# Retention and two feed-forwards on one core: attention of the later blocks split into early and late queries

## The chip, the cores and the metric

The kernel runs on one core of one Trainium2 chip. The metric is the time of one execution on the device in microseconds; a smaller number is better. TensorE multiplies matrices into PSUM, VectorE (DVE) and ScalarE (ACT) work element by element, GpSimd (POOL) does so too but has no access to PSUM, and SyncE (SP) issues the transfers between HBM and SBUF.

## The reference

Four sequences of 576 positions, 8 heads of 64 columns. First comes retention: scores of each query with each earlier key, weighted by a power of a head's gamma that falls with the distance, with no softmax. Its result goes through two feed-forwards over all 2304 positions.

```
scores = q @ k.T / sqrt(64)
Dmat   = where(i >= j, gamma[h] ** (i - j), 0)      # i query, j key
x      = (scores * Dmat) @ v                        # heads side by side: 2304 x 512
h      = x @ w_in;  x = (max(h, 0) + alpha * min(h, 0)) @ w_out          # 512 -> 2048 -> 512
y      = (sigmoid(x @ w_gate) * (x @ w_val)) @ w_out2                    # 512 -> 1536 -> 512
```

Everything is float32 to the reader. The change touches the retention alone.

## The kernel before, in words

**Blocks and chunks.** The 2304 positions are cut into five blocks (`BLOCKS`, L28: 256 positions and four times 512). A sequence is cut at multiples of 128 positions and at the borders of blocks; the pieces are the chunks (`CHUNKS`, L74 to L89), of 128 positions or, at a few borders, 64. Retention is done chunk by chunk. Within a chunk the queries meet the chunk's own keys (the scores); all earlier chunks of the sequence are held in a state of 64 x 64 for each head (`m_sb`), which every chunk reads and then updates.

**A chunk.** Head `2 * pr + e` has its 64 query and key columns in the upper or lower half of the partitions, by `e`; there are four pairs `pr`. GpSimd first scales the queries by powers of gamma (`att_q`, L527) and the values by inverse powers (`att_v`, L535), so that the decay needs no further work. Then TensorE does, as 8 products each:

- the scores (`att_scores`, L571): 128 keys against 128 queries over 64 partitions, so that two heads share the array by rows; VectorE multiplies the two PSUM tiles by the causal mask, once for each `e` (L574);
- the state update `m` (L597): keys times values, into a PSUM tile of its own; VectorE adds it to `m_sb` and scales (L608, L609); left out in the last chunk of a sequence;
- the queries times the old state (L600), into two PSUM tiles `o`; left out in the first chunk of a sequence;
- the masked scores times the values (L611), added into the same `o` tiles.

ScalarE and VectorE then copy `o` to the input `x_t` of the feed-forward. In the trace each of these products is two instructions, so 8 products are 16. Chunks of 64 positions keep two heads in each tile and take a path of their own (L555 for the scores).

**Tiles in PSUM.** From the third block on the two score tiles and the two `o` tiles of a chunk have the same two tags, `a` and `b`, of a pool with one buffer each (`ps_a`): `o` may be written once VectorE has masked the scores. The state update uses the pool `ps_h`, which it shares with the feed-forward.

**Where the chunks stand.** The first two blocks are done in one run at the start (`att_run`), with another pool and one VectorE multiplication for both halves (L564). The chunks of the third to fifth block are put between the steps of the first feed-forward: the main loop takes one stage of `att_stages` at a time, scores and then the rest, with 12 or more matmuls of the feed-forward in between (`for j in range(1, PLAIN)`, L1268). The 13 chunks of these blocks are done from 141 to 264 us; 11 of them have 128 positions. Beside that, VectorE and ScalarE prepare weights for the second feed-forward.

**The order of the work.** TensorE executes in the order in which the program issues (`manual_schedule`, L1493). For the other engines and SyncE's transfers a planner sets the order from its own estimates (`schedule_with_timeline_sim`, L1492); each engine then works strictly in that order. So GpSimd's scaling for a chunk often runs one or two chunks ahead of TensorE, as its load lands.

**Constants.** One array `cst` holds the scaling of the queries, the 128 x 128 mask, the inverse powers, and a 64-wide mask for short chunks, each at a column offset `O_...` (L93 to L98); it is the first load of the program (L502).

Of the kernel before, what the change touches and what calls it, by code (L numbers as in the profile page):

```python
# [10 lines left out]
F32 = mybir.dt.float32  # L11
# [4 lines left out]
ALU = mybir.AluOpType  # L16
# [3 lines left out]
P = 128  # L20
B, H, S, D = 4, 8, 576, 64
NPAIR = H // 2
NT = B * S
DM = 512
# [73 lines left out]
N_CST = O_GK2 + NPAIR  # L98


def constants():
    gamma = (1.0 - 2.0 ** (-5.0 - np.arange(H, dtype=np.float32))).astype(np.float64)
    i = np.arange(P)
    head = 2 * np.arange(NPAIR)[None, :] + (i // D)[:, None]
    out = np.zeros((P, N_CST), np.float32)
    out[:, :O_M] = (gamma[head][:, :, None] ** i / np.sqrt(D)).reshape(P, -1)
    out[:, O_M:O_GK] = i[None, :] >= i[:, None]
    out[:, O_GK:O_GP] = gamma ** -i[:, None].astype(np.float64)
    out[:, O_GP:O_M2] = (gamma[head][:, None, :] ** np.array(LENGTHS)[None, :, None]).reshape(P, -1)

    out[:, O_M2:O_GK2] = i[None, :D] >= i[:, None] % D
    out[:, O_GK2:] = gamma[head] ** -(i[:, None] % D).astype(np.float64)
    return out

# [2 lines left out]
def retention_two_ffn(ctx: ExitStack, tc: tile.TileContext, att, cst, alpha, w1, w2, out0, out1):  # L117
    nc = tc.nc

    const = ctx.enter_context(tc.tile_pool(name="const", bufs=1))  # L120

    big = ctx.enter_context(tc.tile_pool(name="big", bufs=1))
    small = ctx.enter_context(tc.tile_pool(name="small", bufs=2))
# [15 lines left out]
    m_sb = ap.tile([P, NPAIR, D], F32, tag="m", name="m_sb")  # L139
    c_sb = ap.tile([P, N_CST], F32, tag="c", name="c_sb")  # L140
# [21 lines left out]
    mask = c_sb[:, O_M:O_GK]  # L162
    decay = c_sb[:, :O_M].rearrange("p (a i) -> p a i", a=NPAIR)


# [221 lines left out]
    second = []  # L387
# [94 lines left out]
    o = 0  # L482
    for n, (_, _, _, c, _) in enumerate(CHUNKS):
        offset[n] = o
        o += 4 * c * H * D

    def load_chunk(n):
        if n >= len(CHUNKS) or n in raw_a:
            return
        load_qk(n)  # L490
        load_kv(n)

    def load_qk(n):
        if n >= len(CHUNKS):
            return
        c = CHUNKS[n][3]
        half = 2 * c * H * D
# [11 lines left out]
    def load_kv(n):  # L509
        if n >= len(CHUNKS):  # L510
            return
# [17 lines left out]
    def att_v(n):  # L529

        v = raw_a[n][1][:, 1]
        heads = v.shape[1]
        gk = O_GK if heads == H else O_GK2
# [10 lines left out]
    def att_scores(n, pool, tags):  # L544

        c = CHUNKS[n][3]
        qk = raw_a[n][0]
        if c < P:
            if len(tags) == 1:
                ps = pool.tile([P, 2, DM], F32, tag=tags, name=f"s{n}")[:, 0, :NPAIR * c]  # L550
                ps = ps.rearrange("p (a i) -> p a i", a=NPAIR)
            else:
                ps = pool.tile([P, NPAIR, c], F32, tag=tags[0], name=f"s{n}")
            for pr, e in HEADS:
                nc.tensor.matmul(ps[part(e), pr, :], qk[part(e), 1, pr, :], qk[part(e), 0, pr, :], start=True, stop=True)  # L555
            by = c_sb[:, O_M2:O_GK2].unsqueeze(1).to_broadcast([P, NPAIR, c])
            nc.vector.tensor_tensor(out=qk[:, 1], in0=ps, in1=by, op=ALU.mult)
            return qk[part(0), 1], qk[part(1), 1]
        if len(tags) == 1:
            ps = pool.tile([P, 2, DM], F32, tag=tags, name=f"s{n}")  # L560
            for pr, e in HEADS:
                nc.tensor.matmul(ps[:, e, pr * P:(pr + 1) * P], qk[part(e), 1, pr, :], qk[part(e), 0, pr, :], start=True, stop=True)
            s_sb = both_scores[n] = slot([P, 2, NPAIR, P], F32, f"sc{n}")
            nc.vector.tensor_tensor(  # L564
                out=s_sb.rearrange("p e a i -> p (e a) i"), in0=ps.rearrange("p e (a i) -> p (e a) i", a=NPAIR),
                in1=mask.unsqueeze(1).to_broadcast([P, H, c]), op=ALU.mult,
            )
            return s_sb[:, 0], s_sb[:, 1]
        ps = [pool.tile([P, NPAIR, P], F32, tag=tags[e], name=f"s{n}_{e}") for e in range(2)]
        for pr, e in HEADS:  # L570
            nc.tensor.matmul(ps[e][:, pr, :], qk[part(e), 1, pr, :], qk[part(e), 0, pr, :], start=True, stop=True)  # L571
        s_sb = qk[:, 1], small.tile([P, NPAIR, P], F32, tag="s", bufs=3, name=f"sc{n}")
        for e in (1, 0):
            nc.vector.tensor_tensor(  # L574
                out=s_sb[e], in0=ps[e], in1=mask.unsqueeze(1).to_broadcast([P, NPAIR, c]), op=ALU.mult,
            )
        return s_sb

    def att_values(n, s_sb, pool, tags):
# [13 lines left out]
        rows = lambda t, pr, e: kv[part(e), t, pr] if c < P else kv[:, t, 2 * pr + e]  # L593
        if not last:
            m_ps = ps_h.tile([P, NPAIR, D], F32, tag="h", name=f"m{n}")
            for pr, e in HEADS:
                nc.tensor.matmul(m_ps[part(e), pr, :], rows(0, pr, e), rows(1, pr, e), start=True, stop=True)  # L597
        if pos:
            for pr, e in HEADS:
                nc.tensor.matmul(  # L600
                    out(pr, e), m_sb[part(e), pr, :], qk[part(e), 0, pr, :], start=pr < 2, stop=False,
                )
# [7 lines left out]
        for pr, e in HEADS:  # L610
            nc.tensor.matmul(  # L611
                out(pr, e), rows(1, pr, e), s_sb[e][:, pr, :], start=pos == 0 and pr < 2, stop=pr >= 2,
            )
# [606 lines left out]
    late = []  # L1220
# [38 lines left out]
    n = runs_of(2)[0]  # L1259
# [8 lines left out]
    for j in range(1, PLAIN):  # L1268
# [5 lines left out]
        for f in range(first, NF1):  # L1274
# [4 lines left out]
            if j == PLAIN - 1 and staged == total:  # L1279
                if not under_left:  # L1280
# [38 lines left out]
    pool = ctx.enter_context(tc.tile_pool(name="wide", bufs=1, side="right", reuse_waits="tile"))  # L1319
# [110 lines left out]
    ps = [ps_y.tile([P, DM], F32, tag="y", name=f"o0_{e}") for e in range(BLOCKS[0] // P)]  # L1430
    last = None
    for f in range(NF2):
# [4 lines left out]
        g = plain_z(f, ws.pop(f))  # L1437
# [59 lines left out]
```

## Time and profile before

| | us |
|---|---|
| median of 3 runs | 863.33 (863.12 to 864.38) |
| profiled execution | 862.71 |
| its span, first to last instruction | 860.9 |
| TensorE busy in the span | 844.4 |
| VectorE busy | 547.9 |
| ScalarE busy | 419.7 |
| GpSimd busy | 97.3 |

The span is that of the profiled execution; what lies around it is start and end of the program. Busy time is the union of an engine's instructions. Matmuls overlap, so the wall time from the first instruction of a group to the first of the next is what counts in a dense stretch.

### The profile page before, as it was taken

The page shows a single profiled execution, that of the slowest core. Times are in us where ns is not written, and L with a number is a line of the kernel's source. Part 1 is how long each engine was busy: PE and PEld are TensorE (multiplying, and loading weights), DVE is VectorE, ACT ScalarE, POOL GpSimd, SP SyncE. Part 2 cuts the span into 40 slices and gives each one's busy share as a digit, 9 for nine tenths or more (in the row PEclk, how much of TensorE's full clock was granted, in tenths as well). Part 3 has the DMA queues.
Part 4 walks back from the last instruction along what each step waited for, and adds up shares of the span by engine and source line. Part 5 has one row for each costly group of instructions (what it writes and reads, how often), then busy time and mean ns, then how long its engine had stood idle before and what let it go on. Part 6 is the DMA issues. An engine that isn't in the chain of part 4 may idle for free.

```text
span 860.9 us, 13167 instructions
## 1 busy us (share of the span) xinstructions
PE 844.4 (98%) x4898; PEld 704.9 (82%) x4898; DVE 547.9 (64%) x840; ACT 419.7 (49%) x724; POOL 97.3 (11%) x72
## 2 busy tenths in 40 slices
PE   6899999999999999999999999999999999999998
PEld 5798888777778887888888888888888888888897
DVE  4899863785786969997647675469813332695111
ACT  1777754453564769986336653345412222352111
POOL 5357623223100000000000000000000000000000
PEclk9999999999999999999999999999999999999999
DMA  9658999699977125899967999255896561569970
GB/s 341 228 186 274 348 402 365 221 358 407 417 263 280 49 91 194 294 364 346 409 222 274 411 417 407 103 196 192 294 394 228 187 199 69 172 223 371 366 285 26
DMA packets 81728, 234.04 MB, mean 272 GB/s; under 512 B 8576, under 2 KB 9600, under 8 KB 81664
## 3 DMA queue, kind: packets, MB, share of 16 engines
q1 hardware_dynamic: 81664, 233.20, 73.9%
q8 instruction: 39, 0.64, 0.3%
q14 instruction: 25, 0.20, 0.1%
HBM read 169.72 MB, written 63.44 MB: 271 GB/s over the span
## 4 chain that ended last, share of the span: by engine, by line
PE 78%; DVE 1%; DMA 1%; ACT 1%; issue 0%; SPq 0%; DVEq 0%; ACTq 0%
PE a L700 15%; PE yy L700 10%; PE oa L700 8%; PE y L700 6%; PE h L700 5%; PE a_h L700 5%; PE z L700 4%; PE c L700 4%; PE b L700 4%; PE e L700 4%; PE o L700 2%; PE oc L700 2%; PE ob L700 2%; PE oe L700 2%; PE b_h L700 1%; PE c_h L700 1%
## 5 line engine op out<-in xcount | busy, mean ns | idle before, releaser
L700 PE MATMUL h<-x,w 128*128 128x512 f32 (+1 forms) x432 | 84.1, 346 | 2.1 <-DVE t L720 1.3
L700 PEld LDWEIGHTS h<-x,w 128*128 128x128 f32 x432 | 67.5, 190 | 12.6 <-DVE t L720 1.9
L700 PE MATMUL y<-g,w 128*128 128x512 f32 x240 | 58.9, 394 | 0.0
L336 ACT ACTIVATE q<-r 128x512 fp32r<-128x512 f32 x72 | 45.2, 664 | 24.3 <-PE yy L700 9.1
L231 POOL TENSOR_SCALAR r<-r 128x512 int32<-128x512 uint32 x26 | 51.9, 1996 | 42.2 <-DMA r<-w 30.1
L337 DVE TENSOR_TENSOR q<-r,q 128x512 fp32r<-128x512 f32 x72 | 49.3, 709 | 9.7 <-ACT q L336 9.7
L716 ACT ACTIVATE t<-h 128x512 f32<-128x512 f32 (+1 forms) x48 | 25.0, 521 | 57.8 <-PE h L700 57.8
L700 PEld LDWEIGHTS y<-g,w 128*128 128x128 f32 x240 | 44.4, 188 | 10.2 <-issue 1.0
L1029 DVE TENSOR_TENSOR c<-a,es 128x512 f32<-128x512 f32 x24 | 16.7, 699 | 55.3 <-PE a L700 55.3
L229 ACT ACTIVATE r<-r 128x512 f32<-128x512 f32 x68 | 45.0, 669 | 8.2 <-DMA r<-w 6.3
L238 DVE CUSTOM_DVE_ANT_0 r<-r,top 128x1024 uint16<-128x1024 uint16 x52 | 35.6, 696 | 2.3 <-POOL r L231 0.5
L700 PEld LDWEIGHTS z<-x,zp 128*128 128x128 f32 x288 | 36.0, 191 | 0.9
L700 PE MATMUL z<-x,zp 128*128 128x256 f32 x288 | 36.3, 283 | 0.0
L700 PE MATMUL h<-x,v 128*128 128x512 f32 x144 | 35.4, 395 | 0.0
L700 PE MATMUL y<-g,v 128*128 128x512 f32 x144 | 35.2, 393 | 0.0
L700 PEld LDWEIGHTS y<-g,v 128*128 128x128 f32 x144 | 26.7, 188 | 6.1 <-issue 0.7
L700 PE MATMUL a<-xf_1h,tq 128*128 128x512 f32 x96 | 31.5, 389 | 0.0
L700 PE MATMUL e<-xf_5h,tq 128*128 128x512 f32 x96 | 31.5, 389 | 0.0
L700 PE MATMUL a<-xf_6h,tq 128*128 128x512 f32 x96 | 31.5, 389 | 0.0
L700 PE MATMUL b<-xf_2h,tq 128*128 128x512 f32 x96 | 31.5, 389 | 0.0
L700 PE MATMUL a<-xf_7h,tq 128*128 128x512 f32 x96 | 31.5, 389 | 0.0
L700 PE MATMUL c<-xf_3h,tq 128*128 128x512 f32 x96 | 31.5, 389 | 0.0
(468 smaller groups left out, 2130.9 us busy)
## 6 DMA issues: line engine op xcount, KB each, us to landing
tq<-td SPq DMA_DIRECT2D x84, 512.0 KB, 7.1
r<-w SPq DMA_DIRECT2D x68, 512.0 KB, 6.5
wo<-wod SPq DMA_DIRECT2D x42, 512.0 KB, 4.8
v<-w1d SPq DMA_DIRECT2D x40, 512.0 KB, 6.0
td<-q SPq DMA_DIRECT2D x36, 512.0 KB, 5.1
wod<-q SPq DMA_DIRECT2D x24, 512.0 KB, 8.7
zp<-td SPq DMA_DIRECT2D x48, 256.0 KB, 5.8
w1d<-w SPq DMA_DIRECT2D x23, 512.0 KB, 8.5
```

The lines of the kernel that those rows point to most:

```text
L229: nc.scalar.activation(high.bitcast(F32), high.bitcast(F32), AF.Prelu, scale=2.0 ** -112, alpha=2.0 ** 32)
L231: nc.gpsimd.tensor_scalar(low.bitcast(I32), low, 2.0 ** -29, None, ALU.mult)
L238: nc.vector.tensor_tensor(out=out.bitcast(I32), in0=low.bitcast(I32), in1=top.bitcast(I32), op=ALU.add)
L336: nc.scalar.activation(part[0], src, AF.Copy)
L337: nc.vector.tensor_tensor(out=part[1], in0=src, in1=part[0].bitcast(F32), op=ALU.subtract)
L700: nc.tensor.matmul(ps, l, r, start=first and i == 0, stop=last and i == len(todo) - 1, skip_group_check=joins)
L716: nc.scalar.activation(t, ps, AF.Relu)
L1029: nc.vector.tensor_tensor(out=c[q], in0=a[q], in1=es[q], op=ALU.add)
```

## The change

In the chunks of 128 positions from the third block on (`changed_over(n)`), positions 0 to 63 of a chunk are called early and 64 to 127 late.

- Scores: early keys meet all 128 queries, late keys meet the late queries alone. Each product has 64 partitions and 64 key columns, so it takes one quarter of the array; pairs with odd number write late keys to the upper half of the result and early keys to the lower, pairs with even number the other way round. A result tile holds, for two pairs, 3 x 64 columns: early queries of both (each on one half of the partitions), late queries of the even pair, late queries of the odd pair. The mask has 384 columns for each `e` instead of 512.
- Values and keys of odd pairs are loaded with their two halves of positions exchanged, which the host arranges; the inverse powers have a second table for that.
- The part of the values: late queries with all 128 keys (64 columns), then early queries with early keys alone, over 64 partitions, one quarter each.
- The queries times the state come before the state update `m`. GpSimd then sets a word (`tick`) when the last of them is done, and the first early product waits for that.
- The constants get more columns (masks of 4 x 64, one more table of powers; the short chunks use one of these masks).

```diff
+def changed_over(n):
+    return CHUNKS[n][0] > 1 and CHUNKS[n][3] == P
...
-O_GK = O_M + P
-O_GP = O_GK + H
-O_M2 = O_GP + len(LENGTHS) * NPAIR
-O_GK2 = O_M2 + D
+O_GK = O_M + 4 * D
+O_GK1 = O_GK + H
+O_GP = O_GK1 + H
+O_GK2 = O_GP + len(LENGTHS) * NPAIR
...
-            by = c_sb[:, O_M2:O_GK2].unsqueeze(1).to_broadcast([P, NPAIR, c])
+            by = masks[:, 1].unsqueeze(1).to_broadcast([P, NPAIR, c])
...
-                out=s_sb.rearrange("p e a i -> p (e a) i"), in0=ps.rearrange("p e (a i) -> p (e a) i", a=NPAIR),
-                in1=mask.unsqueeze(1).to_broadcast([P, H, c]), op=ALU.mult,
+                out=s_sb.rearrange("p e a (h i) -> p (e a) h i", h=2),
+                in0=ps.rearrange("p e (a h i) -> p (e a) h i", a=NPAIR, h=2),
+                in1=masks[:, 0:3:2].unsqueeze(1).to_broadcast([P, H, 2, D]), op=ALU.mult,
...
-        ps = [pool.tile([P, NPAIR, P], F32, tag=tags[e], name=f"s{n}_{e}") for e in range(2)]
-        for pr, e in HEADS:
-            nc.tensor.matmul(ps[e][:, pr, :], qk[part(e), 1, pr, :], qk[part(e), 0, pr, :], start=True, stop=True)
-        s_sb = qk[:, 1], small.tile([P, NPAIR, P], F32, tag="s", bufs=3, name=f"sc{n}")
+        two = lambda t: t[:, :NPAIR // 2 * 3 * D].rearrange("p (g h i) -> p g h i", g=NPAIR // 2, h=3)
+        flat = lambda t: t.rearrange("p g h i -> p g (h i)")
+        ps = [two(pool.tile([P, DM], F32, tag=tags[e], name=f"s{n}_{e}")) for e in range(2)]
+        for g in range(NPAIR // 2):
+            for late in range(2):
+                for pr, e in HEADS[4 * g:4 * g + 4]:
+                    odd = pr % 2
+                    to = ps[e][part(late ^ odd), g]
+                    queries = qk[part(e), 0, pr, :].rearrange("p (h i) -> p h i", h=2)
+                    nc.tensor.matmul(
+                        to[:, 1 + odd] if late else to[:, 0:2 + odd:1 + odd], qk[part(e), 1, pr, part(late)],
+                        queries[:, 1] if late else queries, start=True, stop=True,
+                    )
...
+        by = c_sb[:, O_M + D:O_M + 4 * D].unsqueeze(1).to_broadcast([P, NPAIR // 2, 3 * D])
         for e in (1, 0):
-            nc.vector.tensor_tensor(
-                out=s_sb[e], in0=ps[e], in1=mask.unsqueeze(1).to_broadcast([P, NPAIR, c]), op=ALU.mult,
-            )
+            nc.vector.tensor_tensor(out=flat(s_sb[e]), in0=flat(ps[e]), in1=by, op=ALU.mult)
...
+        if pos and changed_over(n):
+            a = from_state()
+            fence = nc.gpsimd.memset(tick, 0.0)
+            tc.add_manual_dep(fence.ins, a.ins.name, sync, reason="banks shared by two rows of the array")
         if not last:
             m_ps = ps_h.tile([P, NPAIR, D], F32, tag="h", name=f"m{n}")
             for pr, e in HEADS:
                 nc.tensor.matmul(m_ps[part(e), pr, :], rows(0, pr, e), rows(1, pr, e), start=True, stop=True)
-        if pos:
...
+        if pos and not fence:
+            from_state()
...
+        else:
+            for pr, e in HEADS:
+                nc.tensor.matmul(
+                    out(pr, e)[:, D:], rows(1, pr, e), s_sb[e][:, pr // 2, 1 + pr % 2],
+                    start=pos == 0 and pr < 2, stop=False,
+                )
+            for pr, e in HEADS:
+                at = part(pr % 2)
+                a = nc.tensor.matmul(
+                    out(pr, e)[:, :D], kv[at, 1, 2 * pr + e], s_sb[e][at, pr // 2, 0], start=False, stop=pr >= 2,
+                )
+                if fence and pr == 0:
+                    tc.add_manual_dep(a.ins, fence.ins.name, sync, reason="banks shared by two rows of the array")
...
+            t = t.transpose(1, 0, 2).reshape(P, NPAIR, 2 * D)
+            if changed_over(n):
+                t = np.stack([np.roll(t[:, i], D, axis=0) if i % 2 else t[:, i] for i in range(NPAIR)], axis=1)
+            return t.reshape(P, H * D)
```

`from_state()` is the loop of the queries times the state, as it was.

## Rows read from the trace of the kernel before

**Rows 1.** The page: busy time, share and instructions of TensorE; the transfers.
```profile
PE 844.4 (98%) x4898; PEld 704.9 (82%) x4898; DVE 547.9 (64%) x840; ACT 419.7 (49%) x724; POOL 97.3 (11%) x72
...
DMA packets 81728, 234.04 MB, mean 272 GB/s; under 512 B 8576, under 2 KB 9600, under 8 KB 81664
```

**Rows 2.** Two stretches: length, busy time of each engine, granted clock, transfers.
```profile
200.00:266.00 66.00, 66.00 (x597) 51.27 (x596) 46.37 (x86) 33.45 (x68) 9.57 (x8) 1.00 0.87 336
...
263.60:856.00 592.40, 592.30 (x2747) 495.54 (x2746) 355.78 (x502) 278.31 (x439) 0.00 (x0) 1.00 0.70 255
```

**Rows 3.** TensorE in order of time, one chunk: start, length, instruction, shapes, count.
```profile
140.85 1.16 PE L571 MATMUL s<-qk 64*128 64x128 f32 x16
141.95 3.02 PE L700 MATMUL h<-x,v 128*128 128x512 f32 x12
144.89 0.69 PE L597 MATMUL m<-kv 128*64 128x64 f32 x16
145.51 0.67 PE L600 MATMUL o<-qk,m_sb 64*64 64x128 f32 x16
146.11 0.32 PE L611 MATMUL o<-qk,kv 128*64 128x128 f32 x1
...
146.27 0.27 PE L611 MATMUL o<-qk,kv 128*64 128x128 f32 x1
...
146.38 0.27 PE L611 MATMUL o<-qk,kv 128*64 128x128 f32 x1
...
147.13 0.50 PE L700 MATMUL y<-g,w 128*128 128x512 f32 x1
```

**Rows 4.** The same view of a chunk of 64 positions.
```profile
216.58 0.46 PE L600 MATMUL o<-qk,m_sb 64*64 64x64 f32 x16
216.86 0.41 PE L611 MATMUL o<-qk,kv 64*64 64x64 f32 x16
217.21 0.50 PE L700 MATMUL h<-x,w 128*128 128x512 f32 x1
```

**Rows 5.** VectorE's masks: shortest, median, longest in ns, first and last start.
```profile
L574 DVE TENSOR_TENSOR sc<-s,c_sb x11: 677/684/692, 142.1 to 260.3; 128x512 f32<-128x512 f32 x11
...
L557 DVE TENSOR_TENSOR qk<-s,c_sb x4: 411/420/426, 22.9 to 220.9; 128x256 f32<-128x256 f32 x4
```

**Rows 6.** TensorE and VectorE in order of time in three chunks.
```profile
163.73 0.67 PE L600 MATMUL o<-qk,m_sb 64*64 64x128 f32 x16 [0.32 <-DVE qk L574]
...
195.68 0.69 PE L597 MATMUL m<-kv 128*64 128x64 f32 x16
196.51 0.67 PE L600 MATMUL o<-qk,m_sb 64*64 64x128 f32 x16
...
195.68 0.68 DVE L574 TENSOR_TENSOR qk<-s,c_sb 128x512 f32<-128x512 f32 x1
...
252.51 0.68 DVE L574 TENSOR_TENSOR qk<-s,c_sb 128x512 f32<-128x512 f32 x1
...
252.71 0.69 PE L597 MATMUL m<-kv 128*64 128x64 f32 x16
```

**Rows 7.** GpSimd in order of time: a memset, four of the scalings.
```profile
0.24 0.10 POOL L1485 MEMSET const-float32-0.0<- 128x1 f32 x1 [0.24 <-issue]
...
146.16 1.28 POOL L527 TENSOR_TENSOR qk<-qk,c_sb 128x512 f32<-128x512 f32 x1 [0.48 <-DMA qk<-att]
...
190.19 0.75 POOL L527 TENSOR_TENSOR qk<-qk,c_sb 128x256 f32<-128x256 f32 x1 [5.53 <-DMA qk<-att]
...
206.56 1.28 POOL L527 TENSOR_TENSOR qk<-qk,c_sb 128x512 f32<-128x512 f32 x1 [0.55 <-ACT h L717]
...
224.43 1.29 POOL L535 TENSOR_TENSOR kv<-kv,c_sb 128x512 f32<-128x512 f32 x1 [2.69 <-DVE q L337]
```

**Rows 8.** TensorE in order of time: the start of m in two more chunks.
```profile
186.46 0.69 PE L597 MATMUL m<-kv 128*64 128x64 f32 x16
...
205.12 0.69 PE L597 MATMUL m<-kv 128*64 128x64 f32 x16
```

More of the change, by code (lines that the diff above doesn't have):

```diff
@@ L106, in constants @@
     out[:, :O_M] = (gamma[head][:, :, None] ** i / np.sqrt(D)).reshape(P, -1)
[L107 to L111, printed above, removed]
+    half, at = i // D, i % D
+    causal = at[None, :D] >= at[:, None]
+    second = [np.where(half[:, None] == e, True, causal) for e in range(2)]
+    out[:, O_M:O_GK] = np.concatenate([causal & (half == 0)[:, None], causal, *second], axis=1)
+    by_head = out[:, O_GK:O_GK1] = gamma ** -i[:, None].astype(np.float64)
+    out[:, O_GK1:O_GP] = np.where(np.arange(H) // 2 % 2, np.roll(by_head, D, axis=0), by_head)
+    out[:, O_GP:O_GK2] = (gamma[head][:, None, :] ** np.array(LENGTHS)[None, :, None]).reshape(P, -1)
     out[:, O_GK2:] = gamma[head] ** -(i[:, None] % D).astype(np.float64)
@@ L160, in retention_two_ffn @@
     x2d = [dp.tile([P, KC, nb], F32, tag=f"x2d{j}", name=f"x2d{j}") for j, nb in enumerate(BLOCKS)]
-    mask = c_sb[:, O_M:O_GK]
+    masks = c_sb[:, O_M:O_GK].rearrange("p (h i) -> p h i", h=4)
+    tick = const.tile([P, 1], F32, tag="tick", name="tick")
     decay = c_sb[:, :O_M].rearrange("p (a i) -> p a i", a=NPAIR)
@@ L532, in att_v @@
         heads = v.shape[1]
-        gk = O_GK if heads == H else O_GK2
+        gk = (O_GK1 if changed_over(n) else O_GK) if heads == H else O_GK2
         by = c_sb[:, gk:gk + heads].unsqueeze(2).to_broadcast([P, heads, D])
@@ L564, in att_scores @@
             nc.vector.tensor_tensor(
-                out=s_sb.rearrange("p e a i -> p (e a) i"), in0=ps.rearrange("p e (a i) -> p (e a) i", a=NPAIR),
-                in1=mask.unsqueeze(1).to_broadcast([P, H, c]), op=ALU.mult,
+                out=s_sb.rearrange("p e a (h i) -> p (e a) h i", h=2),
+                in0=ps.rearrange("p e (a h i) -> p (e a) h i", a=NPAIR, h=2),
+                in1=masks[:, 0:3:2].unsqueeze(1).to_broadcast([P, H, 2, D]), op=ALU.mult,
             )
             return s_sb[:, 0], s_sb[:, 1]
-        ps = [pool.tile([P, NPAIR, P], F32, tag=tags[e], name=f"s{n}_{e}") for e in range(2)]
-        for pr, e in HEADS:
-            nc.tensor.matmul(ps[e][:, pr, :], qk[part(e), 1, pr, :], qk[part(e), 0, pr, :], start=True, stop=True)
-        s_sb = qk[:, 1], small.tile([P, NPAIR, P], F32, tag="s", bufs=3, name=f"sc{n}")
+        two = lambda t: t[:, :NPAIR // 2 * 3 * D].rearrange("p (g h i) -> p g h i", g=NPAIR // 2, h=3)
[11 more added lines that the diff above has]
+                    )
+        s_sb = [
+            two(t) for t in
+            (qk[:, 1].rearrange("p a i -> p (a i)"), small.tile([P, DM], F32, tag="s", bufs=3, name=f"sc{n}"))
+        ]
+        by = c_sb[:, O_M + D:O_M + 4 * D].unsqueeze(1).to_broadcast([P, NPAIR // 2, 3 * D])
         for e in (1, 0):
-            nc.vector.tensor_tensor(
-                out=s_sb[e], in0=ps[e], in1=mask.unsqueeze(1).to_broadcast([P, NPAIR, c]), op=ALU.mult,
-            )
+            nc.vector.tensor_tensor(out=flat(s_sb[e]), in0=flat(ps[e]), in1=by, op=ALU.mult)
         return s_sb
@@ L593, in att_values, with from_state @@
         rows = lambda t, pr, e: kv[part(e), t, pr] if c < P else kv[:, t, 2 * pr + e]
+        fence = None
+        sync = mybir.DependencyInfo(mybir.DependencyClass.Sync, mybir.DependencyReason.DATA)
+        def from_state():
+            for pr, e in HEADS:
+                a = nc.tensor.matmul(
+                    out(pr, e), m_sb[part(e), pr, :], qk[part(e), 0, pr, :], start=pr < 2, stop=False,
+                )
+            return a
+        if pos and changed_over(n):
+            a = from_state()
+            fence = nc.gpsimd.memset(tick, 0.0)
+            tc.add_manual_dep(fence.ins, a.ins.name, sync, reason="banks shared by two rows of the array")
         if not last:
@@ L597, in att_values @@
                 nc.tensor.matmul(m_ps[part(e), pr, :], rows(0, pr, e), rows(1, pr, e), start=True, stop=True)
-        if pos:
[L599 to L602, printed above, removed]
+        if pos and not fence:
+            from_state()
         if not last:
@@ L609, in att_values @@
             nc.vector.tensor_tensor(out=m_sb, in0=m_sb if pos else m_ps, in1=by, op=ALU.mult)
[L610 to L613, printed above, removed]
+        if not changed_over(n):
+            for pr, e in HEADS:
+                nc.tensor.matmul(
+                    out(pr, e), rows(1, pr, e), s_sb[e][:, pr, :], start=pos == 0 and pr < 2, stop=pr >= 2,
+                )
+        else:
+            for pr, e in HEADS:
+                nc.tensor.matmul(
+                    out(pr, e)[:, D:], rows(1, pr, e), s_sb[e][:, pr // 2, 1 + pr % 2],
+                    start=pos == 0 and pr < 2, stop=False,
+                )
+            for pr, e in HEADS:
+                at = part(pr % 2)
+                a = nc.tensor.matmul(
+                    out(pr, e)[:, :D], kv[at, 1, 2 * pr + e], s_sb[e][at, pr // 2, 0], start=False, stop=pr >= 2,
+                )
+                if fence and pr == 0:
+                    tc.add_manual_dep(a.ins, fence.ins.name, sync, reason="banks shared by two rows of the array")
         x = x_t[j]
@@ L1451 @@
     parts = []
-    for _, b, pos, c, _ in CHUNKS:
+    for n, (_, b, pos, c, _) in enumerate(CHUNKS):
         def cols(t):
```

1 line of the change is left out of this document (removed).

## The prediction

> **What bounds the kernel now.** I read the page's busy times first, then the stretches, then the order of time around one chunk of attention. TensorE is busy 98% of the span [rows 1]. The stretch that holds nearly all of the changed work, 200 to 266 us, shows it busy 66.00 of 66.00 us, and from 263.6 us to almost the end 592.30 of 592.40, at a granted clock of 1.00 [rows 2]. VectorE has 46 of those 66 us, GpSimd 10. So TensorE's own time is the bound in every stretch behind the first, and a microsecond taken from it at 140 to 264 us comes off the end, as long as nothing makes it wait. What matters is the wall time of each block of TensorE, from its first instruction to the first of the next block, and what could stand in front of it.
>
> **The blocks of a chunk, before.** Eight products of one kind are 16 instructions. In the chunk at 140.85 us [rows 3] the scores take 141.95 - 140.85 = 1.10 us, the state update (m) 0.62, the queries times the state (o from m_sb) 0.60, the values 147.13 - 146.11 = 1.02; between scores and values stand 12 instructions of the feed-forward, 2.94 us. The values go in steps of two instructions, one for each half of the columns, 0.11 us apart (146.27, 146.38): 8 steps of 0.11 are 0.87, so 0.15 us is the change of shape (first weight load exposed, then the drain to the next block). The state products use all four quarters: four steps of 0.11 and 0.15 give the 0.60 measured, so four quarters of 64x64 do run side by side. At 64 columns m gives 8 steps: (0.62 - 0.15) / 8 = 0.06 us a step. The chunk of 64 positions has four quarters at 64 columns: 0.28 us from 216.58 to the next block of the same shape, four steps of 0.06 and 0.05 for the first load, and 0.35 for its values with the drain but no new load [rows 4]. Leaving a shape costs 0.09, entering one 0.05.
>
> **The scores after.** 32 instructions in four quarters: per half of the heads two steps of 128 columns and two of 64. In all 4 x 0.11 + 4 x 0.06 + 0.15 = 0.82 us against 1.10: 0.27 less.
>
> **The values after.** State first, unchanged: 0.60. Then m, followed by late queries of the same shape, so without a drain: 0.05 + 8 x 0.06 = 0.52. Late queries: 8 x 0.06 + 0.09 = 0.56. Early queries, 16 instructions in four quarters: 0.05 + 4 x 0.06 + 0.09 = 0.39. Sum 2.07 against 2.24: 0.17 less. The number of shape changes stays the same, because m and the late queries share one.
>
> **The sum over chunks.** Eleven chunks are changed over. Eight have all four blocks: 8 x (0.27 + 0.17) = 3.5. Two are the last of their sequence, without m, so they have one change of shape more: state and values 1.62 before, 0.60 + 0.61 + 0.39 = 1.60 after; 2 x 0.29 = 0.6. One is first, without state: m and values 1.64 before, 1.47 after, with the scores 0.4. Together 4.5 us less.
>
> A rule of the Trainium skill speaks against it. In the rows four quarter instructions of the state start within one 0.11 us step, and at 64 columns within one of 0.06. The Trainium skill, TensorE: Matmul & The Clock Gate, section "Wait — 56ns, not 53.3ns?", says that starts of matmuls are never closer than about 25 ns. If that held across quarters, a step of four would be 0.10 us and eight small steps per chunk would lose 0.04 each, an estimated 3.6 us in all. The 0.28 us block has 16 instructions, 0.018 each, and decides against it.
>
> **What is put back: state before m.** The state products write the two banks that the masked scores are read from, so they wait for both masks; m, which has a bank of its own, used to cover that. Now they start where m started, and 0.27 earlier. The masks shrink as well: 0.68 us at 512 columns and 0.42 at 256 give 0.55 at 384 [rows 5], two of them 0.26. In most chunks the second mask ends at least 0.8 us before m starts. Three have no such slack [rows 6]. At 195.68 m starts just as the second mask does; it ends at 196.36 and the state follows at 196.51, 0.15 later. After: masks done 196.10, state 196.25 instead of 195.41, a wait of 0.84 where 0.22 was. At 252.71: 252.51 + 0.68 - 0.26 + 0.15 = 253.08 against 252.44, a wait of 0.64 where next to none was. The third, at 163.73, already waits, and gets neither better nor worse. That is 0.62 + 0.62 = 1.2 us. Below it is zero, if VectorE's order moves the masks up; above, if the planner leaves them behind other work in half of the chunks, some 3 us.
>
> **What is put back: the fence.** Ten chunks have it: GpSimd sets one word when the state is done, and the first early product waits for that word. Behind that product on TensorE's queue stand the other early ones and then the feed-forward, so any lateness is TensorE's idle time. The state's last result is there 0.67 us after its first start [rows 3]; a 128x1 memset takes 0.10 [rows 7]; I take the 0.15 from VectorE's end to TensorE's start for GpSimd's too. So 0.92 us from the state's start, against 0.60 + 0.52 + 0.56 = 1.68 until the early products' turn, and 1.21 in the last chunks: hidden by m and the late products, if GpSimd is free. It takes its work in order, and has scaling of queries and values of later chunks (1.3 and 1.0 us each), started as their loads land; the last of it starts at 224.43, so the last four fenced chunks are clear. In the earlier six, a scaling placed ahead of the memset delays it. The trace of before can't show the order. Below: nothing. Above, from three places: a scaling at 146.16 to 147.44 would end the memset at 147.54 and start the early product at 147.69 against 144.62 + 1.68 = 146.30, 1.4 us late; at 190.19, 0.75 long, against 187.87, 3.3; at 206.56, 1.28 long, against 206.53, 1.55 [rows 7, 8]; 6.3 us in all. I take 0.5, nearer to the lower end, since in the order seen most scalings start either well before or well after their chunk's state.
>
> **Smaller edits.** The constants grow by 72 columns, 37 KB ahead of the first queries: 0.14 us at the mean 272 GB/s [rows 1], on the path at the start. The first two blocks keep their instructions, and a mask of the same size. VectorE saves 22 x 0.13 = 2.9 us, which nothing waits for. The keys are changed over before the launch.
>
> **Sum.** 4.5 - 1.2 - 0.5 - 0.1 = 2.7 us. The profiled execution (862.71 us, 1.8 of it around the span) would become 860.0; the median of the runs is 0.6 above it, 863.33, so 860.6 us. Its own range is 859.1 to 861.7. A difference under 0.2%, 1.7 us, can't be told from none here.
>
> **The rivals.** *GpSimd's order:* scalings that wait for their loads stand ahead of the memset in several chunks, and TensorE sits before the early products. For it: loads take several microseconds and GpSimd is often waiting for one; against it: the memset comes first in the program. All three places: 863.3 + 6.3 - 3.2 = 866.4, where 3.2 is the gain without the fence. It turns slower where it costs more than 3.2 us, which the one at 190.19 does alone. *Masks late:* the planner's order leaves VectorE's masks behind other work in half of the chunks, 1 to 2 us more: 862.1, no change. For it: three chunks are there already; against: VectorE is idle 30% of the stretch. *Quarters not side by side* in the new scores and early products: twice the steps, 0.67 + 0.24 = 0.91 us a chunk, 10.0 in all: 870.6. Rows 3 and 4 speak against it. *Split results:* the early products of odd pairs write two runs of 64 columns with a gap; no product of before does. Were these steps twice as long, 4 x 0.11 x 11 = 4.8 us: 865.4, slower from 2.7 us of cost on. Runs of 64 whole words speak against it. The Trainium skill, PSUM — Partial Sum Buffer, "Specifications (TRN2)", says that any access not contiguous slows matmuls significantly; no run here shows it. *Nothing put back* but the constants: 858.9.
>
> **How the numbers follow.** Forecast 0.53, GpSimd's order 0.20 (0.08 of it cheap enough for no change), masks late 0.12, quarters 0.04, split results 0.04, nothing put back 0.07. Faster is most of the forecast and the last: 0.57. No change: the forecast's upper edge, cheap fences, late masks: 0.27. Slower: 0.16. The range goes from just under the best case to 866.0, inside GpSimd's case.
>
> **What would show it.** Scores at 0.82 us and the four blocks at 2.07 with no idle time show the sum right; a scores block near 1.1 shows the quarters or the split results. TensorE's idle time before the state, released by a mask, sizes the first wait; before the early products, released by GpSimd, the second. The prediction is wrong if either sum passes 3 us, or if TensorE starts to wait behind 264 us, where it now never does.

## The result and the profile after

The changed kernel takes 874.34 us (median of 6 runs, 870.57 to 874.80), the kernel before 863.23 us (6 runs, 862.78 to 864.38): a ratio of 1.0115 [1.0093, 1.0137], slower by about 11 us where 2.7 us less was forecast. The profiled execution took 874.8 us, its span is 873.0 us.

The page of the changed kernel, as [rows 1]: TensorE has 352 instructions more and is busy 9.5 us longer; GpSimd has the ten fences more, and the busy times of the other engines and the bytes are within 1% of before.

```profile
PE 853.9 (98%) x5250; PEld 704.9 (81%) x5250; DVE 549.1 (63%) x840; ACT 420.7 (48%) x724; POOL 96.5 (11%) x82
...
DMA packets 81730, 234.11 MB, mean 268 GB/s; under 512 B 8576, under 2 KB 9600, under 8 KB 81664
```

Two stretches of it, as [rows 2]: the attention chunks' last part, and everything behind them.

```profile
200.00:268.00 68.00, 66.15 (x768) 50.97 (x761) 44.84 (x85) 32.95 (x67) 9.93 (x13) 0.97 0.87 332
268.10:869.00 600.90, 600.90 (x2753) 496.17 (x2750) 356.09 (x502) 279.02 (x440) 0.00 (x0) 1.00 0.69 251
```

The second row is the surprise. TensorE never stands still there, at a granted clock of 1.00, yet 2753 matmuls take 600.90 us, 218.3 ns each, where 2747 took 592.40 before, 215.7 ns each. The change doesn't touch these instructions.

The spans of the two profiled executions, cut where the first and the last of the feed-forward's 636 matmuls ahead of the chunks start, and where the first and the last of the 2750 matmuls behind the chunks start ("chunks" is what lies between the two groups; the rest is some 4 us at the end):

```
us            to the first piece   636 matmuls   chunks   2750 matmuls
before              33.10             107.43     123.04      593.38
after               34.34             108.29     125.45      600.95
difference          +1.24              +0.86      +2.41       +7.57
```

**The products themselves** came out as computed. TensorE in order of time, the chunk that answers to [rows 3]:

```profile
142.95 0.90 PE L595 MATMUL s<-qk 64*64 64x128 f32 x32
143.78 3.06 PE L755 MATMUL h<-x,v 128*128 128x512 f32 x12
146.77 0.67 PE L628 MATMUL o<-qk,m_sb 64*64 64x128 f32 x16
147.37 0.69 PE L641 MATMUL m<-kv 128*64 128x64 f32 x16
147.88 0.22 PE L658 MATMUL o<-qk,kv 128*64 128x64 f32 x1
...
148.45 0.27 PE L664 MATMUL o<-qk,kv 64*64 64x64 f32 x1
...
148.84 0.96 PE L755 MATMUL y<-g,w 128*128 128x512 f32 x3
```

Scores 143.78 - 142.95 = 0.83 us (1.10 before), state 0.60, m 0.51, late queries 0.57, early queries 0.39: 2.07 from 146.77 to 148.84, the forecast's number.

**The waits in front of them** did not. The waits of TensorE in the changed kernel that stand at the chunks (total, times, longest):

```profile
PE o L664 <- POOL tick L636: 2.2, 2, 1.7
...
PE o L628 <- DVE qk L605: 0.7, 1, 0.7
PE s L595 <- DVE x L220: 0.5, 1, 0.5
```

GpSimd in order of time at the two fences that were late, and TensorE at the second, from its state products on:

```profile
199.10 0.61 POOL L548 TENSOR_TENSOR kv<-kv,c_sb 128x256 f32<-128x256 f32 x1
199.65 0.10 POOL L636 MEMSET tick<- 128x1 f32 x1
...
207.66 2.65 POOL L540 TENSOR_TENSOR qk<-qk,c_sb 128x512 f32<-128x512 f32 x2 [1.52 <-PE o L628]
210.25 0.10 POOL L636 MEMSET tick<- 128x1 f32 x1
```
```profile
206.95 0.67 PE L628 MATMUL o<-qk,m_sb 64*64 64x128 f32 x16
...
210.41 0.27 PE L664 MATMUL o<-qk,kv 64*64 64x64 f32 x1 [1.70 <-POOL tick L636]
...
210.80 4.61 PE L755 MATMUL y<-g,w 128*128 128x512 f32 x12
```

The state products take 206.95 to 207.55, but the memset stands behind two scalings of 1.3 us. The first of these starts as its load lands: issued at 200.38, that landed at 207.53 by the trace. The `PE o L628` in its row is only the signal that came last; by the program the scaling needs that load and TensorE's work of the chunk before. And TensorE's pause of 1.70 us is followed by a slower array: the pause, and the stretch from 1.4 us behind it, with the granted clock as the third number from the end.

```profile
208.60:210.40 1.80, 0.10 (x4) 0.00 (x0) 1.76 (x3) 1.32 (x3) 1.64 (x3) 1.00 1.00 382
211.80:215.20 3.40, 3.40 (x9) 2.64 (x8) 0.60 (x1) 0.00 (x0) 1.04 (x1) 0.50 0.98 354
```

From 211.8 to 215.2 us the clock is at its lower level, 1.2 GHz, and the 24 matmuls of that block take 1.59 us more than their twins elsewhere.

So the chunks' +2.41 us, from the blocks of TensorE (first instruction to first of the next; a wait is what a block has over the shortest of its kind): products -4.46, fences +2.31, clock +1.59, waits for masks and for the copies of `o` +2.82 where 0.61 was, and the rest, some 0.8, for the feed-forward's matmuls in between, which are slower as those behind are.

### The profile page after: what moved, and what is told of

The parts are those of the page before. It is cut to its first block, busy times and chain, and to the rows that moved or that the text cites. A ratio compares the mean times of both kernels' runs of the same rounds, so it can differ in the third digit from the quotient of the medians.

```text
span 873.0 us, 13866 instructions
## 1 busy us (share of the span) xinstructions
PE 853.9 (98%) x5250; PEld 704.9 (81%) x5250; DVE 549.1 (63%) x840; ACT 420.7 (48%) x724; POOL 96.5 (11%) x82
## 4 chain that ended last, share of the span: by engine, by line
PE 79%; DVE 2%; POOL 0%; issue 0%; ACT 0%; DVEq 0%; POOLq 0%
PE a L755 15%; PE yy L755 10%; PE oa L755 8%; PE y L755 6%; PE h L755 5%; PE a_h L755 5%; PE z L755 4%; PE e L755 4%; PE c L755 4%; PE b L755 4%; PE o L755 2%; PE oe L755 2%; PE ob L755 2%; PE oc L755 2%; PE c_h L755 1%; PE b_h L755 1%
## 5 line engine op out<-in xcount | busy, mean ns | idle before, releaser
L755 PE MATMUL y<-g,w 128*128 128x512 f32 x240 | 60.7, 403 | 0.0
L244 POOL TENSOR_SCALAR r<-r 128x512 int32<-128x512 uint32 x26 | 49.2, 1892 | 45.3 <-DMA r<-w 22.5
L755 PE MATMUL a<-xf_4h,tq 128*128 128x512 f32 x96 | 31.8, 392 | 0.0
```

Of the source, the lines that this page charges most:

```text
L244: nc.gpsimd.tensor_scalar(low.bitcast(I32), low, 2.0 ** -29, None, ALU.mult)
L755: nc.tensor.matmul(ps, l, r, start=first and i == 0, stop=last and i == len(todo) - 1, skip_group_check=joins)
```

## The experiments

Where a kernel's products differ from the change it is said so; otherwise all compute the same. "Dense" is the time of the 2750 matmuls behind the chunks in the profiled execution.

**e1 and e2: the new word's place.** `tick` is one more tile in a pool of constants, 4 bytes a partition. In the compiled program's allocation it takes 32 bytes, and 878 of the large tiles, allotted from the same side of SBUF, begin 32 bytes higher (`m_sb` at 190752 and not 190720); those allotted from the other side stay. e1 makes the tile 64 bytes; e2 gives the tile to the kernel before, which has no use for it.

```diff
-    tick = const.tile([P, 1], F32, tag="tick", name="tick")
+    tick = const.tile([P, 16], F32, tag="tick", name="tick")
```


> The changed kernel with the fence's word in a tile of 64 bytes a partition instead of 4; orders of all engines are the same. Theory (addresses): the 4-byte tile took 32 bytes in front of all tiles on the left side of SBUF, while those on the right side stayed; the matmuls of the feed-forwards that take one operand from each side start 230 to 236 ns apart instead of 227. Then this kernel's 2750 matmuls behind attention take 593.8 us again instead of 601.3, the stretch before attention 0.9 less, and the whole about 9 us less than the changed kernel: 861.5 to 865.5 us, by whether TensorE's clock falls once or not. Rival (order): the planner's other order of VectorE, ScalarE and transfers slows the matmuls; then it stays at 870 to 875 us, and the distance stays at 230 to 236 ns.

Measured: 870.74 us (869.56 to 873.01), 1.0089 [1.0076, 1.0103]; dense 599.16.

```diff
+    tick = const.tile([P, 1], F32, tag="tick", name="tick")
+    nc.gpsimd.memset(tick, 0.0)
```


> The kernel before with a tile of 4 bytes a partition behind the other small constants, set once at the start and not used; attention is as before. Theory (addresses): 8 to 9 us slower than before, 871 to 872.5 us, with the 2750 matmuls behind attention at about 601 us. Rival (order, or the new attention itself): no change, 862.5 to 864 us.

Measured: 872.02 us (871.60 to 873.13), 1.0096 [1.0082, 1.0111]; dense 600.97. Four bytes that nobody reads cost the kernel before 8.4 us (its median beside these runs was 863.58). The address was the cause, but e1 missed: it isn't alignment to 64 bytes that is wanted.

One group of the same product, from 300 to 850 us, in the kernel before and in e2 (count, busy us, mean ns of one):

```profile
L700 PE MATMUL a<-xf_7h,tq 128*128 128x512 f32 x96 | 31.5, 389 | 0.0
```
```profile
L702 PE MATMUL a<-xf_7h,tq 128*128 128x512 f32 x96 | 32.0, 394 | 0.0
```

**e3 and e8: both sides.** `pad_sb` is the first tile on the other side; its length moves that side. e3 lengthens it and so moves that side down by 32 bytes, away from the moved tiles; e8 shortens it, and both sides go up by 32.

```diff
-    pad_sb = pad.tile([P, 184], F32, tag="pad", name="pad_sb")
+    pad_sb = pad.tile([P, 192], F32, tag="pad", name="pad_sb")    # e3; 176 in e8
```


> The changed kernel with its 4-byte tile, but with the filler at the right end of SBUF 32 bytes larger, so that the tiles on the right lie 32 bytes off a multiple of 64 as those on the left do. Theory (addresses, relative): only the difference between the two operands counts; as with the 64-byte tile, 861.5 to 865.5 us, and the matmuls 227 ns apart. Rival (addresses, absolute): an operand that is not at a multiple of 64 bytes costs by itself; then all are slow and it is slower than the changed kernel, 875 us or more. Rival (order): 870 to 875.

Measured: 871.47 us (868.84 to 874.09), 1.0091 [1.0075, 1.0107]; dense 599.15, e1's number.

> The changed kernel with its 4-byte tile, and the filler 32 bytes smaller, so that the tiles on the right move up by the same 32 bytes as those on the left: the distance between any two big tiles is that of the kernel before, though no tile lies at a multiple of 64. Theory (distance alone counts): equal to e5_word_in_pad within 1 us, 227 ns apart. Rival (absolute address): 870 us or more.

Measured: 864.94 us (862.14 to 867.56), 1.0018 [1.0003, 1.0033]; dense 593.68, the kernel before's. Every large tile has moved and the dense part loses nothing: only the distance between the two sides counts. e3 has the same distance as e1, 64 bytes, and the same dense time. The same group in e1 and in e8:

```profile
L755 PE MATMUL a<-xf_7h,tq 128*128 128x512 f32 x96 | 31.8, 392 | 0.0
```
```profile
L755 PE MATMUL a<-xf_7h,tq 128*128 128x512 f32 x96 | 31.5, 389 | 0.0
```

With the addresses of the compiled programs beside the traces, the time from one 512-column matmul's start to the next can be sorted by a distance: address of the columns that the matmul streams, less the address of the weights of the next matmul, which are loaded beside it. Over all kernels up to e8:

```
distance mod 256 bytes      0      32      64     192     224
mean start to start, ns   227.8  233.4   229.1   232.9   233.2
```

Before, all 2407 such pairs of the dense part have distance 0 (mean 226.8). After, 911 don't and take 233.3; the other 1496 take 228.0. Together that is (911 x 6.5 + 1496 x 1.2) ns = 7.7 us, the 7.57 lost. The 256 of the table is a way to sort, not a measured period: in the kernel before all these distances are multiples of 512, the shifts tried are 32 and 64 bytes either way, and no run has 128 or 256. The distance to a matmul's own weights differs from that to the next one's in only 66 pairs, too few to say which counts. That a read of the stream and the weight load get in each other's way would fit it, but no run separates that from other causes; the distance is what was shown.

**e5: the word in the padding.** With `pad_sb`'s first word as `tick` every address is as before.

```diff
-    tick = const.tile([P, 1], F32, tag="tick", name="tick")
+    tick = pad_sb[:, 0:1]
```


> The changed kernel, with the fence's word in the filler tile at the right end of SBUF: every tile lies where it lay in the kernel before, and all orders are those of the changed kernel. Theory (distance of the two operands): in the runs so far matmuls start 227 ns apart where the moving operand and the next weights have the same address modulo 256, and 229 to 233 where not; the 64-byte tile left 911 of 2407 pairs unequal. Here all are equal: the 2750 matmuls take 593.8 us, 7.5 less than in the changed kernel, the stretch before attention 0.9 and that between the chunks 0.5 less; 862 to 866 us, where the waits for the fence and the clock are as in the changed kernel. Rival (order of the other engines): stays at 870 or more.

Measured: 865.63 us (863.57 to 867.42, 12 runs), 1.0026 [1.0015, 1.0037]; dense 593.60. Of the 11 us 8.7 are gone, and what the forecast reasoned about is left: still 2.3 us slower, not 2.7 faster. The waits of TensorE for the fence in this kernel:

```profile
PE o L664 <- POOL pad_sb L636: 3.4, 2, 3.0
```

In its chunks (126.32 us against 123.04) 3.57 us are lost at fences and 1.64 to a clock of 0.50 from 211.9 to 215.3, again right after the pause.

**e4 and e6: GpSimd's order.** The scalings for the next chunk are put behind this chunk's fence, in e4 with e1's 64-byte tile, in e6 with e5's word.

```diff
+            fenced.append(fence)
...
-                att_q(n + 1)
-                att_v(n + 1)
+                with ExitStack() as stack:
+                    if fenced:
+                        stack.enter_context(tc.issue_after(fenced[-1].ins))
+                    att_q(n + 1)
+                    att_v(n + 1)
```


> The 64-byte tile, and in addition GpSimd's scalings for the next chunk are put behind the fence of this chunk. Theory: the two waits for the fence (0.5 and 1.8 us in the changed kernel's profile) go, and with the longer one the fall of TensorE's clock behind it (1.7 us in a block of 24 matmuls); 3 to 4 us less than with the 64-byte tile alone where that one's clock falls: 860.5 to 862.5 us. Rival: the waits for the masks and the start eat the gain anyway; then it is equal to the 64-byte tile within 1 us.

Measured: 872.63 us (869.08 to 875.82), 1.0103 [1.0085, 1.0122].

> As e5_word_in_pad, and GpSimd's scalings for the next chunk stand behind this chunk's fence. Theory: the fence's waits (2.3 us in the changed kernel) are gone, and what hangs on them of the clock; 860 to 863 us, 2 to 3 less than e5_word_in_pad. Rival: it costs elsewhere, since the planner's order changes; within 1 us of e5_word_in_pad.

Measured: 865.51 us (859.95 to 867.64, 12 runs), 1.0021 [1.0004, 1.0037]. The profiled execution is the shortest, 859.95: no wait for a fence, no fall of the clock, chunks 120.94 us. The fence waits are gone in e4's profile too, yet e4 is no faster than e1 and e6 no faster than e5. In e4 another wait had taken their place, TensorE's for the last chunk's mask:

```profile
266.78 1.58 PE L629 MATMUL o<-qk,m_sb 64*64 64x128 f32 x16 [6.79 <-DVE qk L606]
```

**e7: the state behind m again.** e6 with `m` ahead of the state products, as before the change.

```diff
-        if pos and changed_over(n):
-            a = from_state()
-            fence = nc.gpsimd.memset(tick, 0.0)
...
+        if pos:
+            a = from_state()
+        if pos and changed_over(n):
+            fence = nc.gpsimd.memset(tick, 0.0)
```


> As e6_pad_fence_first, with the state update m before the queries times the state, as in the kernel before. Theory: the waits for the masks (about 2 us in the changed kernel) go, for one more change of shape in eight chunks (8 x 0.14 = 1.1 us), and the fence is covered by the late queries alone (1.21 us against 0.92 needed): about 1 us less than e6_pad_fence_first. Rival: the fence, now less covered, waits in several chunks, and it is slower than e6_pad_fence_first by 1 us or more.

Measured: 864.01 us (860.29 to 869.99), 1.0015 [0.9994, 1.0037]. A change of shape more costs 0.15 us in each of eight chunks (`m` 0.62 and late queries 0.62, where it was 0.51 and 0.57), and TensorE still waited 1.8 us at one mask. Its median is 1.5 us below e6's, less than either kernel's own spread; it is no faster than the kernel before, so what m covers is at most a part of what is missing.

**e9 and e10: repeats**, one profile each, of the kernel before and of e6.

> The kernel before once more, for its profile alone. Theory: the fall of TensorE's clock at 26 to 31 us, which the profiles of the changed kernel and of most others show and the first profile of before does not, belongs to the start and not to the change; it shows here too, or not, by chance, and from 141 us on everything is as in the first profile (2750 matmuls in 593.4 us, 123.0 us from the end of the first stretch to them). Rival: the fall belongs to the change, and before never has it.

Measured: 863.26 us; no fall of the clock in this profile. The mean clocks of the other runs speak against the rival: of 92 runs of the kernel before beside these experiments, 70 have a granted clock below 1.000, so it falls there too, by chance; where in the run they don't tell.

> The kernel of e6_pad_fence_first once more, for its profile: its first profile (859.95 us) is the fastest of its 12 runs, whose median is 865.5. Theory: in the slower runs VectorE's mask of a late chunk stands behind an operation that waits for a load of weights (b from w1f), as in e4_fence_first, where this took 6.9 us; 864 to 867 us here, with TensorE waiting some us for a mask. Rival: the clock alone, one or two falls of 1.7 us each.

Measured: 866.23 us, and this pair of e6 and e10, one kernel with two times, points at the cause. VectorE in order of time, e6 and then e10: the subtraction of a later weight's preparation, which needs the load `b<-w1f`, what is queued behind it, the masks of the last chunk; then TensorE there.

```profile
251.46 0.41 DVE L651 TENSOR_TENSOR m_sb<-m_sb,m 128x256 f32<-128x256 f32 x1
253.36 0.69 DVE L379 TENSOR_TENSOR s<-b 128x512 f32<-128x512 f32 x1 [1.49 <-DMA b<-w1f]
...
257.77 0.55 DVE L606 TENSOR_TENSOR qk<-s,c_sb 128x384 f32<-128x384 f32 x1
```
```profile
258.38 1.12 PE L629 MATMUL o<-qk,m_sb 64*64 64x128 f32 x16
```
```profile
251.86 0.41 DVE L651 TENSOR_TENSOR m_sb<-m_sb,m 128x256 f32<-128x256 f32 x1
257.33 0.69 DVE L379 TENSOR_TENSOR s<-b 128x512 f32<-128x512 f32 x1 [5.06 <-DMA b<-w1f]
...
261.74 0.55 DVE L606 TENSOR_TENSOR qk<-s,c_sb 128x384 f32<-128x384 f32 x1
```
```profile
262.35 0.96 PE L629 MATMUL o<-qk,m_sb 64*64 64x128 f32 x8 [3.59 <-DVE qk L606]
```

The DMA engines had no room from 200 to 240 us, e6 first, transfers in the last two numbers (share, GB/s):

```profile
200.00:240.00 40.00, 40.00 (x435) 31.11 (x435) 27.98 (x47) 19.90 (x41) 8.55 (x10) 1.00 1.03 411
```
```profile
200.00:240.00 40.00, 40.00 (x429) 31.19 (x432) 27.78 (x47) 19.51 (x40) 8.55 (x10) 1.00 1.01 385
```

At a full share the rate was 411 GB/s in one execution and 385 in the other, and the load was issued at 246.46 and 250.11 us and landed some 7 us later in both (253.34 and 257.31). So the later issue is what made VectorE wait longer; that the lower rate delayed the issue was not tested. In the kernel before the same subtraction waits as well, but for 0.39 us, and TensorE gets there later:

```profile
256.05 0.69 DVE L366 TENSOR_TENSOR s<-b 128x512 f32<-128x512 f32 x1 [0.39 <-DMA b<-w1f]
...
260.94 0.68 DVE L574 TENSOR_TENSOR qk<-s,c_sb 128x512 f32<-128x512 f32 x1
```

And in e10 the clock is at half from that pause on, for 6.8 us (261.8 to 268.6), twice as long as in the changed kernel:

```profile
262.35:268.60 6.25, 6.25 (x55) 4.93 (x56) 5.19 (x8) 4.36 (x8) 0.10 (x1) 0.50 0.67 232
```

**e11 and e12: the fence on ScalarE**, in e12 with m ahead of the state besides.

```diff
-            fence = nc.gpsimd.memset(tick, 0.0)
+            fence = nc.scalar.activation(tick, na_sb[:, 0:1], AF.Copy)
```


> As e5_word_in_pad, with the fence's word written by ScalarE, which has no operation that waits for the attention's loads, in place of GpSimd. Theory: the wait for the fence falls from 3.6 us in e5_word_in_pad to under 0.7, and the clock falls less often; 861 to 863.5 us. Rival: ScalarE's fence stands behind its weight preparation in several chunks and waits as long; 865 or more.

Measured: 866.35 us (861.57 to 871.29, 12 runs), 1.0036 [1.0015, 1.0056].

> As e11_fence_on_act, with the state update m before the queries times the state, as in the kernel before. Theory: the waits for the masks go (2.3 us in e6_pad_fence_first) for one more change of shape in eight chunks (1.1 us): about 1 us faster than e11_fence_on_act, 860 to 862.5 us. Rival: the fence has only the late queries as cover and waits in most chunks; slower than e11_fence_on_act.

Measured: 866.77 us (861.18 to 869.87, 12 runs), 1.0028 [1.0010, 1.0045]. The waits for the fence are gone here too. In the profiles VectorE stood 7.66 and 3.75 us at that load, TensorE up to 6.2 and 2.7 us at a mask, with the clock at 0.50 for 6.8 us from 263 on in both. Wherever the fence is, the load stays.

**e13, e14 and e15: the masks out from behind the load.** The generator that prepares these sums makes one step more before its first subtraction, which then stands behind the last chunk's masks in VectorE's order. e13 is e6 with that line, e14 the kernel before with it, e15 is e5 with it.

```diff
     def prepare_sums(t):
 
+        yield
         b, s = raw_w.pop((1, t))
```


> The kernel with the word in pad_sb and the scalings behind the fence (e6), but the generator that prepares the sums of a later weight makes one step more before it begins, so that its first subtraction stands in VectorE's order behind the last attention chunk's masks and no longer ahead of them. In e10 and e11 VectorE stood 5.1 and 7.7 us at that subtraction for the load b<-w1f, with the masks of the last chunk behind it, and TensorE 3.6 and 6.2 us for the mask. Theory (the gain of attention is held back by that load, through VectorE's order): TensorE's waits on the line of the o matmuls with m_sb fall below 2.5 us together in 245 to 265 us, the clock stays above 0.997, and the median is 860.0 to 863.0 us, 0.5 to 3 below the kernel before. Rival (the work of the sums is needed as early as before, so the wait moves): 864.5 to 867 us as e6, with a new wait of TensorE of 3 us or more for w, y or s tiles between 255 and 300 us.

Measured: 860.51 us (859.17 to 861.12, 7 runs), 0.9963 [0.9945, 0.9980]; the only kernel that beats the one before, by 2.7 us. Its chunks take 119.57 us, 3.47 less than before, and the view of TensorE's waits lists none for a mask or a fence. VectorE goes from the state straight on:

```profile
251.85 0.41 DVE L652 TENSOR_TENSOR m_sb<-m_sb,m 128x256 f32<-128x256 f32 x1
252.29 0.42 DVE L653 TENSOR_TENSOR m_sb<-m_sb,c_sb 128x256 f32<-128x256 f32 x1
...
255.85 0.56 DVE L607 TENSOR_TENSOR qk<-s,c_sb 128x384 f32<-128x384 f32 x1 [1.34 <-PE s L597]
```

The masks now wait for the scores, as they should, and end at 256.87 where e10's ended at 262.76. The preparation, now at 282 us for the second weight, makes nothing late: dense 593.54.

> The kernel before with the same extra step in the generator of the sums and nothing else. Its trace shows VectorE waiting for the second load of these only 0.4 us, and TensorE 0.3 us for a mask. Theory (before, attention ends late enough that the load is hidden): 862.8 to 863.8 us, no change that can be told. Rival (the extra step helps or hurts any kernel): below 862.3, or above 864.5 as later loads find their buffers later.

Measured: 863.50 us (862.01 to 864.53, 11 runs), 1.0004 [0.9995, 1.0012]: without the change the line gives nothing.

> The change with its word in pad_sb (e5, every address as before) and the extra step in the generator of the sums; the fence stays behind GpSimd's scalings. Theory: e5 took 865.6; what is left are the fence waits of 2 to 3.5 us and the clock's fall of about 1.6 us, the masks of the last chunk cost at most 1 us: 862.0 to 864.5. Rival (the load is no part of it): 865 to 867 as e5.

Measured: 864.87 us (862.42 to 866.18, 11 runs), 1.0014 [1.0001, 1.0026], above the range of the theory. With the fence still behind the scalings its waits alone eat the gain (4.16 us over the shortest blocks), whatever the masks do:

```profile
PE o L665 <- POOL pad_sb L637: 4.0, 2, 2.3
...
PE o L629 <- DVE qk L606: 0.9, 1, 0.9
```

So two waits in a row hold back the chunks, and taking away one of them (e6 or e15) shows the other.

## Why the prediction was wrong

The step that failed first is the bold **Smaller edits**, and with it the **Sum**: it priced the constants' 72 columns by their transfer, 0.1 us, and gave the new word no cost but its memset. No term said that one more tile moves the operands of 2750 matmuls. That is +7.57 us behind the chunks and 0.8 between them (e2, e5, e8), three quarters of the loss. It was not among the rivals either. The sign by which the text would have called itself wrong, TensorE waiting behind 264 us, did not come: these matmuls don't wait, they are each a little longer. Only a count over time, as [rows 2] allowed, shows that.

Going through its other steps:

- *Scores, values, sum over chunks:* right. 0.83 and 2.07 us, and -4.46 against the 4.5 forecast. *Quarters not side by side* and *Split results* are refuted: 32 instructions of the scores in 0.83 us, written in two runs of 64 columns for odd pairs. The Trainium skill's rule for accesses that are not contiguous (PSUM — Partial Sum Buffer, "Specifications (TRN2)") did not show in this pattern.
- *State before m:* 1.2 taken. The waits for masks came to 1.94 us (0.81 and 0.23 in front of the state at 166.1 and 257.2, and 0.45 inside each of the two), against 0.61 before, so about 1.3 net: right in size, and half right in place. Of the two chunks named, the one at 252.71 (now 257.2) lost 0.68 where 0.64 was forecast, and the one at 195.68 nothing. The third, at 163.73 (now 166.1), was to get neither better nor worse, and lost 1.26 where 0.40 was. The 0.45 was not foreseen: the state block goes on with the first mask's bank and waits in the middle for the second. A further 0.88 us at 161.18, scores waiting for VectorE's copy of `o`, was not considered.
- *The fence:* 0.5 taken, 2.31 measured, 3.57 in e5 and 4.16 in e15. The rival *GpSimd's order* had the right mechanism, and the upper bound by [rows 7, 8] one of its places: the third, 1.55 us there and 1.77 measured, at the fence of 210.25. The other, 0.54, stood at a chunk that the bound doesn't name, and its first two places had no wait. The bound put one scaling of 1.28 us ahead of the memset; it was two in one run, 2.65 us, behind a load that landed at 207.53.
- *The clock:* no term. In the changed kernel a pause of 1.70 us at the chunks is followed by 3.4 us at half the clock, a loss of 1.6; [rows 2] showed 1.00 in a kernel that does not pause there, and the sum took that as given. It isn't the rule: pauses of 1.77 us in e1 and e8, and one of 2.3 us in e15, brought no fall; 3.0 us in e5 and 2.7 to 6.8 us in e4, e10, e11 and e12 did.
- *"a microsecond taken from it ... comes off the end":* wrong for the place. VectorE's wait of 0.39 us for a load, in front of masks that TensorE needed 6 us later, was a bound close behind TensorE. Once TensorE was early it ended last (e4, e10 to e12), with e13 as the proof.

With the addresses kept, the fence ahead of the scalings and the masks ahead of the load, the change gives 2.7 us by the medians, 1.7 to 4.7 by the interval of the ratio. That this equals the forecast is no support for it: the forecast was for the kernel without these three edits, and netted other costs.

What stays open: why a shift of one side by 32 or 64 bytes slows the matmul, and which distances do; why the transfers' rate differs at a full share, and what decides whether the clock falls after a pause: near the start TensorE waits some 2 us for `m_sb` in the kernel before and in the changed one (until 26.5 and 27.3 us), and of these two profiles only the latter, with most of the experiments', has the clock at half from about 27 us on, for 3.4 us or more. By the mean clocks given at e9 the kernel before falls in most of its runs too, so a part of what the changed kernel's profile loses ahead of the chunks is likely chance.

## What to carry to other kernels

When a change adds a tile, however small, compare the addresses of the large operands before and after, and count matmuls against time in a stretch that the change leaves alone: a busy share of 100% hides a slower instruction. Where TensorE gets faster, list each wait of the other engines that is short today in front of something that TensorE needs, for these become the bound; one edit that removes one of two such waits shows no gain. A fence on an engine with a queue of its own is as late as what is queued ahead of it, so say what that is.

## What the hardware showed that was not expected

- A 512-column matmul of this kernel starts 226.8 ns after the one before it where the distance of streamed columns and next weights is that of the kernel before, a multiple of 512 bytes, and 229 to 233 ns where one of the two is shifted by 32 or 64 bytes; 0.9% of the whole time hung on it.
- The granted clock was at 0.50, the lower of its two levels, for 3.4 us from 1.4 us after a pause of TensorE of 1.70 us on (the changed kernel), and for 6.8 us from within a pause of 3.6 us on (e10), so such a pause cost nearly twice its length; other pauses of 1.8 to 2.3 us (e1, e3, e7, e8, e15) brought no fall.
- Sixteen instructions in four quarters of the array, 64 columns each, start within 0.24 us (210.41 to 210.65).
